# A layernorm, dilated-attention and gated-MLP kernel: logits matmuls issued in pairs, a second PSUM bank pair for the down projection, and weight loads in 27 pieces

## Chip, cores, metric

One core of one Trainium2 chip. The time is device microseconds of one execution. The granted TensorE clock is listed with every run and plays a part below. All runs here count as fast; where it matters I split them further, by granted clock: 0.999 or 1.000 ("full clock") and 0.994 or 0.995 ("dropped").

## The reference, cut to what matters

Both branches take the layernorm of the same x, and the result is their sum with x. S = 2048, D = 640, F = 1536, 32 heads of 20, a window of 8 positions at distance 2.

```python
x = A_x
xn = _layernorm(x, axis=-1)
return x + _A_ref(xn, A_wqkv, A_wo) + _B_ref(xn, B_w_gate, B_w_up, B_w_down)

# _A_ref, per head: each position looks at itself and 7 earlier ones, 2 apart
logits = jnp.einsum("bhsd,bhswd->bhsw", q, kg) * scale      # kg, vg: gathered k, v
attn = _softmax(jnp.where(mask, logits, -1e9), axis=-1)
o = jnp.einsum("bhsw,bhswd->bhsd", attn, vg)                # then @ wo
# _B_ref: no activation
h = (xn @ w_gate) * (xn @ w_up);  out = h @ w_down
```

## The kernel before

A small scheduler lists operations in program order for each engine and derives the semaphore waits from what each reads and writes. An engine works through its own list in order. The work is one long list for TensorE: QKV; then logits steps, with gate and up groups of the MLP between them; then softmax, with more gate/up groups and the first four down tiles beside it; then PV, with the rest of the MLP between its matmuls; then a tail.

VectorE multiplies Q by a shifted K (`qk_prod`, three buffers). TensorE sums the products over each head with four matmuls against a 0/1 matrix of 32 columns, one for each quarter of S, each in its own 32 columns of the array:

```python
def qk_logits(w, c, slot):
    lb = 6 + (w % 2)
    for jj in range(NJ):                       # NJ = 4
        ... e.matmul(PS[32 * jj:32 * jj + 32, lb, :], G[:, c, :],
                     PRODW[:, slot, jj * JB:(jj + 1) * JB],
                     start=(c == 0), stop=(c == NCH - 1), tile_position=(0, 32 * jj))
# the logits stage: 40 steps, one gate or up group (5 matmuls of 128x128x512) after each
qk_prod(order[0][0], order[0][1], 0)
for i, (w, c) in enumerate(order):
    if i + 1 < len(order):
        w2, c2 = order[i + 1]
        qk_prod(w2, c2, (i + 1) % NPW)         # NPW = 3
    qk_logits(w, c, i % NPW)
    next_glu()
```

A down tile (24 matmuls, 640 columns out) always uses PSUM banks 4 and 5. Ahead of PV, ScalarE empties them (`bev`, L552) into a buffer that shares its memory with the softmax's sums:

```python
def glu_down_q(st, jg, q):                     # cut
    ... e.matmul(PS[:, 4, :], HT4[:, hb, m, rows], WD[:, m, 0:512], ...)      # q = 0, 1
    ... e.matmul(PS[:, 5, 0:128], HT4[:, hb, m, rows], WD[:, m, 512:D], ...)  # q = 2
def glu_xb(st, jg):                            # cut
    if not pv_started[0]:
        ... e.activation(xbl(t), b_view(), ACT.Copy)     # b_view(): banks 4 and 5
    else:
        ... e.tensor_tensor(xbl(t), b_view(), XST[:, slot, :], ALU.add)
# softmax: five pieces, five MLP groups after each
for pc in softmax_pieces():
    pc()
    for _ in range(5):
        next_glu()
```

The MLP and output weights are four loads, issued after the first quarter of QKV.

Of the kernel before, what the change touches and what calls it, by code (L numbers as in the profile page):

```python
# [7 lines left out]
ALU = mybir.AluOpType  # L8
# [3 lines left out]
D = 640  # L12
# [166 lines left out]
def psk(b):  # L179
    return [("ps", b, q) for q in range(4)]  # L180


def build_kernel(nc, A_x, A_wqkv, A_wo, B_x, B_w_gate, B_w_up, B_w_down, out, dbg=None):
# [34 lines left out]
    def xbl(t):  # L218
        return XBL_LO[:, t, :] if t < 8 else XBL_HI[:, t - 8, :]
# [21 lines left out]
    def tp_view(u):  # L241
        return PS[:, u, :].bitcast(BF16)[:, 0:NCH * 128].rearrange("p (c f) -> p c f", c=NCH)

    def b_view():
        return PS[:, 4:6, :].rearrange("p a f -> p (a f)")[:, 0:D]

    xhbm = A_x[0]
    ohbm = out[0]
# [43 lines left out]
                                                      wqkv_src[:, :, g3 * D:(g3 + 1) * D]))(g3),  # L292
               writes=[("wqkv", g3)], lane=f"sp_wqkv{g3}", name=f"ld_wqkv{g3}")

    def glu_weight_loads():
        op("sp", lambda e: e.dma_start(WG[:], B_w_gate.rearrange("(c p) n -> p c n", p=128)),
           writes=[("wg",)], lane="sp_wg", name="ld_wg")
        op("sp", lambda e: e.dma_start(WU[:], B_w_up.rearrange("(c p) n -> p c n", p=128)),
           writes=[("wu",)], lane="sp_wu", name="ld_wu")
        op("sp", lambda e: e.dma_start(WD[:], B_w_down.rearrange("(c p) n -> p c n", p=128)),  # L300
           writes=[("wd",)], lane="sp_wd", name="ld_wd")
        op("sp", lambda e: e.dma_start(WO[:], A_wo.rearrange("(c p) n -> p c n", p=128)),
           writes=[("wo",)], lane="sp_wo", name="ld_wo")

    def ln_stats(t):
        slot = t % NXS
# [153 lines left out]
    def g_bank(k):  # L460
        if pv_started[0]:
            return 2
        if ktx_free[0]:
            return (2, 3, 1, 6)[k % 4]
        return (2, 3, 1)[k % 3]

    def e_bank(i):
# [2 lines left out]
    def u_bank(k):  # L470
        if pv_started[0]:
            return (4, 5)[k % 2]
        if ktx_free[0]:
            return (4, 5, 7, 0)[k % 4]
        return (4, 5, 0)[k % 3]

    def slots(k):
        if ktx_free[0]:
# [3 lines left out]
    def glu_gate(m, jg):  # L482
        k = glu_pair[0]
        gb = g_bank(k)
        gsx, usx, gk, uk, extra = slots(k)
        gs = k % NGX
        for c in range(NCH):
            op("pe", (lambda c: lambda e: e.matmul(PS[:, gb, :], WG[:, c, m * 128:(m + 1) * 128],  # L488
                                                 XNT[:, c, jg * JB:(jg + 1) * JB],
                                                 start=(c == 0), stop=(c == NCH - 1)))(c),  # L490
               reads=[("wg",), ("xnt", c, jg)], writes=psk(gb), name=f"gate{m}_{jg}_{c}")
        op("act", lambda e: e.activation(gsx[:, gs, :], PS[:, gb, :], ACT.Copy),  # L492
           reads=psk(gb) + extra, writes=[gk], name=f"gev{m}_{jg}")

    h_pending = []
    H_DEFER = 2

    def flush_h(keep=0):
        while len(h_pending) > keep:
            h_pending.pop(0)()  # L500

    def flush_h_block(jg):
        flush_h()

    def glu_up(m, jg):
        k = glu_pair[0]
        glu_pair[0] += 1
        ub = u_bank(k)
        gsx, usx, gk, uk, extra = slots(k)
        gs = k % NGX  # L510
        hb = jg % 2
        for c in range(NCH):
            op("pe", (lambda c: lambda e: e.matmul(PS[:, ub, :], WU[:, c, m * 128:(m + 1) * 128],  # L513
                                                 XNT[:, c, jg * JB:(jg + 1) * JB],
                                                 start=(c == 0), stop=(c == NCH - 1)))(c),
               reads=[("wu",), ("xnt", c, jg)], writes=psk(ub), name=f"up{m}_{jg}_{c}")
        if pv_started[0]:
            op("dve", lambda e: e.tensor_copy(usx[:, gs, :], PS[:, ub, :]),
               reads=psk(ub) + extra, writes=[uk], name=f"ucp{m}_{jg}")
        else:  # L520
            op("act", lambda e: e.activation(usx[:, gs, :], PS[:, ub, :], ACT.Copy),  # L521
               reads=psk(ub) + extra, writes=[uk], name=f"uev{m}_{jg}")

        def h_op(m=m, jg=jg, gs=gs, hb=hb, gsx=gsx, usx=usx, gk=gk, uk=uk):
            op("dve", lambda e: e.tensor_tensor(HT4[:, hb, m, :], usx[:, gs, :], gsx[:, gs, :], ALU.mult),
               reads=[uk, gk, ("ra",)], writes=[("ht", hb, m)], name=f"h{m}_{jg}")
        h_pending.append(h_op)
        flush_h(keep=H_DEFER)

    def glu_down_q(st, jg, q):  # L530
        hb = jg % 2
        t = 4 * jg + st
        rows = slice(st * 128, (st + 1) * 128)
        if q < 2:
            for m in range(6 * q, 6 * q + 6):
                op("pe", (lambda m: lambda e: e.matmul(PS[:, 4, :], HT4[:, hb, m, rows], WD[:, m, 0:512],  # L536
                                                     start=(m == 0), stop=(m == NF - 1)))(m),
                   reads=[("ht", hb, m), ("wd",)], writes=psk(4), name=f"down{t}_0_{m}")
        else:
            for m in range(NF):  # L540
                op("pe", (lambda m: lambda e: e.matmul(PS[:, 5, 0:128], HT4[:, hb, m, rows], WD[:, m, 512:D],  # L541
                                                     start=(m == 0), stop=(m == NF - 1)))(m),
                   reads=[("ht", hb, m), ("wd",)], writes=psk(5), name=f"down{t}_1_{m}")

    xb_constructed = set()

    def glu_xb(st, jg):
        t = 4 * jg + st
        slot = t % NXS
        xb_constructed.add(t)  # L550
        if not pv_started[0]:
            op("act", lambda e: e.activation(xbl(t), b_view(), ACT.Copy),  # L552
               reads=psk(4) + psk(5) + xbl_alias_keys(t), writes=[("xbl", t)], name=f"bev{t}")
            op("dve", lambda e: e.tensor_tensor(xbl(t), xbl(t), XST[:, slot, :], ALU.add),
               reads=[("xbl", t), ("xst", slot)], writes=[("xbl", t)], name=f"xb{t}")
        else:
            op("dve", lambda e: e.tensor_tensor(xbl(t), b_view(), XST[:, slot, :], ALU.add),  # L557
               reads=psk(4) + psk(5) + [("xst", slot)] + xbl_alias_keys(t), writes=[("xbl", t)], name=f"xb{t}")

    units = [(w, c, j) for j in range(NJ) for c in range(NCH) for w in range(W)]  # L560
    unit_idx = {u: i for i, u in enumerate(units)}
# [36 lines left out]
    def wo_half(t, nb):  # L598
        j = t // 4
        u = t % 2  # L600
        rows = slice(t * TS, (t + 1) * TS)
        cols = slice(nb * DHALF, (nb + 1) * DHALF)
        if pv_all_issued[0]:
            ab = (ABANK, 0, 3)[wo_ctr[0] % 3]
        else:
            ab = ABANK
        wo_ctr[0] += 1
        for c in range(NCH):
            op("pe", (lambda c: lambda e: e.matmul(PS[:, ab, 0:DHALF], QOT[:, c, rows], WO[:, c, cols],  # L609
                                                 start=(c == 0), stop=(c == NCH - 1)))(c),  # L610
               reads=[("ot", c, j), ("wo",)], writes=psk(ab), name=f"wo{t}_{nb}_{c}")
        op("dve", lambda e: e.tensor_tensor(FOUT[:, u, cols], PS[:, ab, 0:DHALF], xbl(t)[:, cols], ALU.add),
           reads=psk(ab) + [("xbl", t)], writes=[("fout", u, nb)], name=f"fin{t}_{nb}")
        if nb == 1:
            op("sp", lambda e: e.dma_start(ohbm[rows, :], FOUT[:, u, :]),
               reads=[("fout", u, 0), ("fout", u, 1)], writes=[("hbm", t)],
               lane=f"sp_fin{u}", name=f"odma{t}")
# [5 lines left out]
    def ln_tile_pre(t):  # L623
        ln_stats(t)
        g = ln_scalars(t, t + 1)
        ln_apply(t, g)
        if t + 8 < NT:
            x_load(t + 8)

    def ln_tile_pe(t):  # L630
        pe_tr(t)
# [14 lines left out]
    for j in range(NJ):  # L646
# [8 lines left out]
                dump("qt0", QOT[:, :, 0:JB], [("qt", c, 0) for c in range(NCH)])  # L655
                dump("kt0", KTP[:, :, 0:PAD + JB], [("kt", c, 0) for c in range(NCH)] + [("kt", c, -1) for c in range(NCH)])
        if j == 0:
            glu_weight_loads()
    for t in pend_pre:
        ln_tile_pre(t)  # L660
    for t in pend_pe:
# [17 lines left out]
    def add_dn(jg):  # L679
        for st in range(4):  # L680
            glu_groups.append(("dn", st, jg, 0))
            glu_groups.append(("dn", st, jg, 1))
            glu_groups.append(("dn", st, jg, 2))

    add_pairs(0)
    add_pairs(1)
    add_dn(0)
# [6 lines left out]
    def run_glu(it):  # L694
        k = it[0]
        if k == "xr":
            x_reload(it[1])
            return 0.0
        if k == "gate":
            glu_gate(it[1], it[2]); return 1.1  # L700
        if k == "up":
            glu_up(it[1], it[2]); return 1.1
        if k == "dn":
            flush_h_block(it[2])
            glu_down_q(it[1], it[2], it[3])
            if it[3] == 2:
                glu_xb(it[1], it[2])
                return 0.7
            return 1.3
        return 0.0  # L710
# [9 lines left out]
                return r  # L720
        return None

    step = 0
    order = [(w, c) for w in range(W) for c in range(NCH)]
    qk_prod(order[0][0], order[0][1], 0)
    for i, (w, c) in enumerate(order):
        if i + 1 < len(order):
            w2, c2 = order[i + 1]
            qk_prod(w2, c2, (i + 1) % NPW)
        qk_logits(w, c, i % NPW)  # L730
        next_glu()
    ktx_barrier()

    dump("logits", LOG[:, :, :].rearrange("p w s -> p (w s)"), [("log", w, j) for w in range(W) for j in range(NJ)])
# [112 lines left out]
```

## Time and profile before

| | before |
|---|---|
| time, median of 4 runs | 361.0 us (360.43 to 362.96) |
| span of the profiled run, granted clock | 358.3 us, 1.000 |
| TensorE busy | 338.2 us (94%) |
| first QKV matmul | 16.09 us |
| logits stage: first logits matmul (85.46) to the end of its 40 groups (145.98) | 60.52 us |
| softmax stage, to the first PV matmul (178.85) | 32.87 us |
| PV, to its last matmul (338.81) | 159.96 us |
| tail, to the end | 19.49 us |

TensorE is busy 94% of the time, so a change helps only where TensorE stands idle or where its matmuls stand further apart than their work needs. The prediction below shows the lines for this: a table of stretches, the timeline of the logits stage, and the holes between down tiles.

### The profile page before, as it was taken

How to read it: one execution, taken by the hardware profiler on the slowest of the kernel's cores; microseconds unless marked ns; L12 is line 12 of the kernel's file. 1: busy time of each engine (PE TensorE's matmuls, PEld its weight loads, DVE VectorE, ACT ScalarE, POOL GpSimd, SP SyncE). 2: the span in 40 equal slices, each digit the busy share in tenths (PEclk: the TensorE clock that was granted, in tenths of full speed). 3: DMA queues.
4: the chain of work that ended last, by engine and by line, in shares of the span. 5: the costliest groups of instructions: out<-in, count | busy, mean ns of one | idle time of the engine just before them, and what ended most of it. 6: DMA issues, size and time to landing. Idle time of an engine off the chain costs nothing.

```text
span 358.3 us, 4796 instructions
## 1 busy us (share of the span) xinstructions
PE 338.2 (94%) x1884; PEld 158.8 (44%) x1884; DVE 212.5 (59%) x439; ACT 202.8 (57%) x362; POOL 16.6 (5%) x43
## 2 busy tenths in 40 slices
PE   1499999999999999978999999999999999999996
PEld 1245454444333333434444445554445444555553
DVE  5746440033999998635475676556667676656633
ACT  4467676554444444561477776556776777556400
POOL 7000000002000200001100000000000000000000
PEclk9999999999999999999999999999999999999999
DMA  7929900002000110001100000111000100010011
GB/s 217 307 69 399 340 4 0 0 2 65 8 2 0 33 43 2 0 0 38 37 1 2 0 0 20 54 40 37 0 20 18 38 2 0 1 38 18 20 37 38
DMA packets 10982, 17.47 MB, mean 49 GB/s; under 512 B 928, under 2 KB 9120, under 8 KB 10960
## 3 DMA queue, kind: packets, MB, share of 16 engines
q1 hardware_dynamic: 10096, 14.42, 11.9%
q0 software_dynamic: 864, 2.75, 2.5%
q8 instruction: 15, 0.25, 0.3%
q14 instruction: 7, 0.06, 0.1%
HBM read 14.42 MB, written 2.62 MB: 48 GB/s over the span
## 4 chain that ended last, share of the span: by engine, by line
PE 91%; DVE 5%; ACT 3%; DMA 1%; issue 1%; DVEq 0%; ACTq 0%
PE PS L355 19%; PE PS L488 15%; PE PS L513 14%; PE PS L536 11%; PE PS L573 10%; PE PS L589 10%; PE PS L609 5%; PE PS L380 4%; PE PS L541 3%; ACT LOG L413 1%; PE PS L340 1%; DVE KTP L557 1%; DVE STATS L308 1%; DVE STATS L310 1%; DMA XST<-in_A_x_dram 1%; DVE PRODW L416 1%
## 5 line engine op out<-in xcount | busy, mean ns | idle before, releaser
L575 ACT ACTIVATE ES<-PS 128x512 bf16<-128x512 f32 x160 | 88.3, 598 | 39.5 <-PE PS L573 39.5
L581 DVE TENSOR_TENSOR PB<-ES,VTP 128x512 bf16<-128x512 bf16 x160 | 67.1, 424 | 56.6 <-ACT ES L575 52.6
L355 PE MATMUL PS<-XNT,RA 128*128 128x512 bf16 x300 | 68.2, 385 | 1.1 <-DVE XNT L346 1.1
L374 DVE TENSOR_TENSOR PRODW<-QOT,KTP 128x2048 bf16<-128x2048 bf16 x40 | 48.8, 1225 | 31.2 <-ACT KTP L368 19.6
L573 PE MATMUL PS<-LOG,GTZ 128*128 128x512 bf16 x160 | 60.5, 379 | 0.0
L589 PE MATMUL PS<-PB,IDENT 128*128 128x512 bf16 x160 | 60.5, 379 | 0.0
L513 PE MATMUL PS<-XNT,WU 128*128 128x512 bf16 x240 | 59.8, 380 | 0.0
L488 PE MATMUL PS<-XNT,WG 128*128 128x512 bf16 x240 | 59.8, 380 | 0.0
L536 PE MATMUL PS<-WD,RA 128*128 128x512 bf16 x192 | 46.1, 379 | 4.7 <-ACT PRODW L552 4.2
L355 PEld LDWEIGHTS PS<-XNT,RA 128*128 128x128 bf16 x300 | 29.2, 99 | 35.0 <-issue 3.2
L513 PEld LDWEIGHTS PS<-XNT,WU 128*128 128x128 bf16 x240 | 21.9, 98 | 28.0 <-issue 4.5
L488 PEld LDWEIGHTS PS<-XNT,WG 128*128 128x128 bf16 x240 | 21.8, 98 | 27.9 <-issue 4.5
L536 PEld LDWEIGHTS PS<-WD,RA 128*128 128x128 bf16 x192 | 18.4, 98 | 26.6 <-ACT PRODW L552 4.7
L609 PE MATMUL PS<-WO,QOT 128*128 128x320 bf16 x160 | 27.0, 299 | 0.1
L492 ACT ACTIVATE KTP<-PS 128x512 bf16<-128x512 f32 x28 | 16.7, 597 | 11.8 <-PE PS L488 11.8
L589 PEld LDWEIGHTS PS<-PB,IDENT 128*128 128x128 bf16 x160 | 15.6, 98 | 17.1 <-DVE PB L581 2.3
L573 PEld LDWEIGHTS PS<-LOG,GTZ 128*128 128x128 bf16 x160 | 15.6, 98 | 15.3 <-ACT ES L575 0.3
L492 ACT ACTIVATE ES<-PS 128x512 bf16<-128x512 f32 x20 | 11.9, 597 | 16.4 <-PE PS L488 16.4
L521 ACT ACTIVATE PB<-PS 128x512 bf16<-128x512 f32 x20 | 11.9, 597 | 16.4 <-PE PS L513 16.4
L609 PEld LDWEIGHTS PS<-WO,QOT 128*128 128x128 bf16 x160 | 15.5, 98 | 10.7 <-ACT QOT L592 0.5
L340 PE MATMUL PS<-IDENT,XNS 128*128 128x128 bf16 x80 | 8.4, 247 | 11.4 <-ACT XNS L332 11.4
L332 ACT ACTIVATE XNS<-XST,NB,RSTD 128x640 bf16<-128x640 bf16 x16 | 14.7, 919 | 6.8 <-DVE NB L324 6.8
(61 smaller groups left out, 246.6 us busy)
## 6 DMA issues: line engine op xcount, KB each, us to landing
XST<-in_A_x_dram SPq DMA_DIRECT2D x16, 160.0 KB, 3.6
XST<-in_A_x_dram POOLq DMA_DIRECT2D x16, 160.0 KB, 2.5
out_dram<-FOUT SPq DMA_DIRECT2D x16, 160.0 KB, 1.8
RA<-in_A_wqkv_dram SPq DMA_DIRECT2D x3, 800.0 KB, 10.4
WG<-in_B_w_gate_dram SPq DMA_DIRECT2D x1, 1920.0 KB, 9.0
WU<-in_B_w_up_dram SPq DMA_DIRECT2D x1, 1920.0 KB, 13.4
WD<-in_B_w_down_dram SPq DMA_DIRECT2D x1, 1920.0 KB, 18.3
WO<-in_A_wo_dram SPq DMA_DIRECT2D x1, 800.0 KB, 19.7
```

The source lines that it names most:

```text
L332: op("act", lambda e: e.activation(XNS[:, u, :], XST[:, slot, :], ACT.Identity, bias=NB[:, t:t + 1], scale=RSTD[:, t:t + 1]), reads=[("xst ...
L355: op("pe", (lambda c: lambda e: e.matmul(PS[:, kb, :], WQKV[:, c, m * 128:(m + 1) * 128], XNT[:, c, j * JB:(j + 1) * JB], start=(c == 0), ...
L374: op("dve", lambda e: e.tensor_tensor(PRODW[:, slot, :], QOT[:, c, :], KTP[:, c, lo:lo + S], ALU.mult), reads=rk, writes=[("prod", slot)], ...
L488: op("pe", (lambda c: lambda e: e.matmul(PS[:, gb, :], WG[:, c, m * 128:(m + 1) * 128], XNT[:, c, jg * JB:(jg + 1) * JB], start=(c == 0), ...
L492: op("act", lambda e: e.activation(gsx[:, gs, :], PS[:, gb, :], ACT.Copy), reads=psk(gb) + extra, writes=[gk], name=f"gev{m}_{jg}")
L513: op("pe", (lambda c: lambda e: e.matmul(PS[:, ub, :], WU[:, c, m * 128:(m + 1) * 128], XNT[:, c, jg * JB:(jg + 1) * JB], start=(c == 0), ...
L536: op("pe", (lambda m: lambda e: e.matmul(PS[:, 4, :], HT4[:, hb, m, rows], WD[:, m, 0:512], start=(m == 0), stop=(m == NF - 1)))(m), reads ...
L573: op("pe", lambda e: e.matmul(PS[:, eb, :], GTZ[:, j, c, :], LOG[:, w, :], start=True, stop=True), reads=[("gtz", j)] + [("log", w, jq) fo ...
L575: op("act", lambda e: e.activation(ES[:, es, :], PS[:, eb, :], ACT.Copy), reads=psk(eb), writes=[("es", es)], name=f"Eev{w}_{c}_{j}")
L581: op("dve", lambda e: e.tensor_tensor(PB[:, pb, :], ES[:, es, :], VTP[:, c, lo:lo + JB], ALU.mult), reads=rk, writes=[("pb", pb)], name=f" ...
L589: op("pe", lambda e: e.matmul(PS[:, ob, :], IDENT[:], PB[:, pb, :], start=(w == 0), stop=(w == W - 1)), reads=[("ident",), ("pb", pb)], wr ...
L609: op("pe", (lambda c: lambda e: e.matmul(PS[:, ab, 0:DHALF], QOT[:, c, rows], WO[:, c, cols], start=(c == 0), stop=(c == NCH - 1)))(c), re ...
```

## The change

Four intentions: logits two by two, so that the array changes less often between 32-column and 128-column matmuls, with products issued two steps ahead; a second bank pair (6 and 7) for every other down tile, ahead of PV and in the tail; three banks each for gate and up where there were four; and the weights in 27 pieces, early, between the x loads. A function that interleaves down tiles with gate/up, and a flag that holds back h multiplies, are added but never used.

```diff
-    def b_view():
-        return PS[:, 4:6, :].rearrange("p a f -> p (a f)")[:, 0:D]
+    def b_view(bb):
+        return PS[:, bb:bb + 2, :].rearrange("p a f -> p (a f)")[:, 0:D]
...
-    def glu_weight_loads():                          # 4 loads
+    wchunks = [...]                                  # 5 + 5 + 12 + 5 loads
+    def weight_chunk_loads(n):
...
     def g_bank(k):                                   # u_bank likewise
-        if ktx_free[0]:
-            return (2, 3, 1, 6)[k % 4]
         return (2, 3, 1)[k % 3]
+    def b_banks(t):
+        if t not in b_banks_of:
+            b_banks_of[t] = (6 if pv_all_issued[0] and t % 2 else 4) if pv_started[0] else (4 if t % 2 else 6)
+        return b_banks_of[t]
...
         if t + 8 < NT:
             x_load(t + 8)
+            weight_chunk_loads(3)
...
     qk_prod(order[0][0], order[0][1], 0)
+    qk_prod(order[1][0], order[1][1], 1)
     for i, (w, c) in enumerate(order):
-        if i + 1 < len(order):
-            w2, c2 = order[i + 1]
-            qk_prod(w2, c2, (i + 1) % NPW)
+        if i + 2 < len(order):
+            w2, c2 = order[i + 2]
+            qk_prod(w2, c2, (i + 2) % NPW)
         qk_logits(w, c, i % NPW)
-        next_glu()
+        if i % 2 == 1:
+            next_glu()
+            next_glu()
```

More of the change, by code (lines that the diff above doesn't have):

```diff
@@ L293, in weight_loads @@
                writes=[("wqkv", g3)], lane=f"sp_wqkv{g3}", name=f"ld_wqkv{g3}")
-    def glu_weight_loads():
-        op("sp", lambda e: e.dma_start(WG[:], B_w_gate.rearrange("(c p) n -> p c n", p=128)),
-           writes=[("wg",)], lane="sp_wg", name="ld_wg")
-        op("sp", lambda e: e.dma_start(WU[:], B_w_up.rearrange("(c p) n -> p c n", p=128)),
-           writes=[("wu",)], lane="sp_wu", name="ld_wu")
-        op("sp", lambda e: e.dma_start(WD[:], B_w_down.rearrange("(c p) n -> p c n", p=128)),
-           writes=[("wd",)], lane="sp_wd", name="ld_wd")
-        op("sp", lambda e: e.dma_start(WO[:], A_wo.rearrange("(c p) n -> p c n", p=128)),
-           writes=[("wo",)], lane="sp_wo", name="ld_wo")
+    wchunks = []
+    wg_src = B_w_gate.rearrange("(c p) n -> p c n", p=128)
+    wu_src = B_w_up.rearrange("(c p) n -> p c n", p=128)
+    wd_src = B_w_down.rearrange("(c p) n -> p c n", p=128)
+    wo_src = A_wo.rearrange("(c p) n -> p c n", p=128)
+    for c in range(NCH):
+        wchunks.append((("wg", c), (lambda c: lambda e: e.dma_start(WG[:, c, :], wg_src[:, c, :]))(c)))
+        wchunks.append((("wu", c), (lambda c: lambda e: e.dma_start(WU[:, c, :], wu_src[:, c, :]))(c)))
+    for m in range(NF):
+        wchunks.append((("wd", m), (lambda m: lambda e: e.dma_start(WD[:, m, :], wd_src[:, m, :]))(m)))
+    for c in range(NCH):
+        wchunks.append((("wo", c), (lambda c: lambda e: e.dma_start(WO[:, c, :], wo_src[:, c, :]))(c)))
+    def weight_chunk_loads(n):
+        while n > 0 and wchunks:
+            key, fn = wchunks.pop(0)
+            op("sp", fn, writes=[key], lane=f"sp_{key[0]}{key[1]}", name=f"ld_{key[0]}{key[1]}")
+            n -= 1
     def ln_stats(t):
@@ L472, in u_bank @@
             return (4, 5)[k % 2]
-        if ktx_free[0]:
-            return (4, 5, 7, 0)[k % 4]
         return (4, 5, 0)[k % 3]
+    b_banks_of = {}
+    def b_banks(t):
+        if t not in b_banks_of:
+            b_banks_of[t] = (6 if pv_all_issued[0] and t % 2 else 4) if pv_started[0] else (4 if t % 2 else 6)
+        return b_banks_of[t]
     def slots(k):
@@ L490, in glu_gate @@
                                                  start=(c == 0), stop=(c == NCH - 1)))(c),
-               reads=[("wg",), ("xnt", c, jg)], writes=psk(gb), name=f"gate{m}_{jg}_{c}")
+               reads=[("wg", c), ("xnt", c, jg)], writes=psk(gb), name=f"gate{m}_{jg}_{c}")
         op("act", lambda e: e.activation(gsx[:, gs, :], PS[:, gb, :], ACT.Copy),
@@ L496, in build_kernel @@
     H_DEFER = 2
+    h_hold = [False]
     def flush_h(keep=0):
@@ L515, in glu_up @@
                                                  start=(c == 0), stop=(c == NCH - 1)))(c),
-               reads=[("wu",), ("xnt", c, jg)], writes=psk(ub), name=f"up{m}_{jg}_{c}")
+               reads=[("wu", c), ("xnt", c, jg)], writes=psk(ub), name=f"up{m}_{jg}_{c}")
         if pv_started[0]:
@@ L527, in glu_up @@
         h_pending.append(h_op)
-        flush_h(keep=H_DEFER)
+        if not h_hold[0]:
+            flush_h(keep=H_DEFER)
     def glu_down_q(st, jg, q):
@@ L533, in glu_down_q @@
         rows = slice(st * 128, (st + 1) * 128)
+        bb = b_banks(t)
         if q < 2:
             for m in range(6 * q, 6 * q + 6):
-                op("pe", (lambda m: lambda e: e.matmul(PS[:, 4, :], HT4[:, hb, m, rows], WD[:, m, 0:512],
+                op("pe", (lambda m: lambda e: e.matmul(PS[:, bb, :], HT4[:, hb, m, rows], WD[:, m, 0:512],
                                                      start=(m == 0), stop=(m == NF - 1)))(m),
-                   reads=[("ht", hb, m), ("wd",)], writes=psk(4), name=f"down{t}_0_{m}")
+                   reads=[("ht", hb, m), ("wd", m)], writes=psk(bb), name=f"down{t}_0_{m}")
         else:
             for m in range(NF):
-                op("pe", (lambda m: lambda e: e.matmul(PS[:, 5, 0:128], HT4[:, hb, m, rows], WD[:, m, 512:D],
+                op("pe", (lambda m: lambda e: e.matmul(PS[:, bb + 1, 0:128], HT4[:, hb, m, rows], WD[:, m, 512:D],
                                                      start=(m == 0), stop=(m == NF - 1)))(m),
-                   reads=[("ht", hb, m), ("wd",)], writes=psk(5), name=f"down{t}_1_{m}")
+                   reads=[("ht", hb, m), ("wd", m)], writes=psk(bb + 1), name=f"down{t}_1_{m}")
     xb_constructed = set()
@@ L550, in glu_xb @@
         xb_constructed.add(t)
+        bb = b_banks(t)
         if not pv_started[0]:
-            op("act", lambda e: e.activation(xbl(t), b_view(), ACT.Copy),
-               reads=psk(4) + psk(5) + xbl_alias_keys(t), writes=[("xbl", t)], name=f"bev{t}")
+            op("act", lambda e: e.activation(xbl(t), b_view(bb), ACT.Copy),
+               reads=psk(bb) + psk(bb + 1) + xbl_alias_keys(t), writes=[("xbl", t)], name=f"bev{t}")
             op("dve", lambda e: e.tensor_tensor(xbl(t), xbl(t), XST[:, slot, :], ALU.add),
@@ L556, in glu_xb @@
         else:
-            op("dve", lambda e: e.tensor_tensor(xbl(t), b_view(), XST[:, slot, :], ALU.add),
-               reads=psk(4) + psk(5) + [("xst", slot)] + xbl_alias_keys(t), writes=[("xbl", t)], name=f"xb{t}")
+            op("dve", lambda e: e.tensor_tensor(xbl(t), b_view(bb), XST[:, slot, :], ALU.add),
+               reads=psk(bb) + psk(bb + 1) + [("xst", slot)] + xbl_alias_keys(t), writes=[("xbl", t)],
+               name=f"xb{t}")
     units = [(w, c, j) for j in range(NJ) for c in range(NCH) for w in range(W)]
@@ L610, in wo_half @@
                                                  start=(c == 0), stop=(c == NCH - 1)))(c),
-               reads=[("ot", c, j), ("wo",)], writes=psk(ab), name=f"wo{t}_{nb}_{c}")
+               reads=[("ot", c, j), ("wo", c)], writes=psk(ab), name=f"wo{t}_{nb}_{c}")
         op("dve", lambda e: e.tensor_tensor(FOUT[:, u, cols], PS[:, ab, 0:DHALF], xbl(t)[:, cols], ALU.add),
@@ L657, in build_kernel @@
         if j == 0:
-            glu_weight_loads()
+            weight_chunk_loads(len(wchunks))
     for t in pend_pre:
@@ L683, in add_dn, with add_dn_interleaved @@
             glu_groups.append(("dn", st, jg, 2))
+    def add_dn_interleaved(jg, jn):
+        glu_groups.append(("hold", True))
+        for st in range(4):
+            for q in range(3):
+                glu_groups.append(("dn", st, jg, q))
+            glu_groups.append(("gate", st, jn))
+            glu_groups.append(("up", st, jn))
+        glu_groups.append(("hold", False))
+        for st in range(4):
+            glu_groups.append(("xr", 4 * jn + st))
+        for m in range(4, NF):
+            glu_groups.append(("gate", m, jn))
+            glu_groups.append(("up", m, jn))
     add_pairs(0)
@@ L698, in run_glu @@
             return 0.0
+        if k == "hold":
+            h_hold[0] = it[1]
+            if not it[1]:
+                flush_h()
+            return 0.0
         if k == "gate":
@@ L703, in run_glu @@
         if k == "dn":
-            flush_h_block(it[2])
+            if not h_hold[0]:
+                flush_h_block(it[2])
             glu_down_q(it[1], it[2], it[3])
@@ L721, in next_glu @@
         return None
-    step = 0
     order = [(w, c) for w in range(W) for c in range(NCH)]
     qk_prod(order[0][0], order[0][1], 0)
+    qk_prod(order[1][0], order[1][1], 1)
     for i, (w, c) in enumerate(order):
-        if i + 1 < len(order):
-            w2, c2 = order[i + 1]
-            qk_prod(w2, c2, (i + 1) % NPW)
+        if i + 2 < len(order):
+            w2, c2 = order[i + 2]
+            qk_prod(w2, c2, (i + 2) % NPW)
         qk_logits(w, c, i % NPW)
-        next_glu()
+        if i % 2 == 1:
+            next_glu()
+            next_glu()
     ktx_barrier()
```

## The prediction

> **What bounds the kernel now.** I read the page first (busy shares and the 40 slices), then a table of stretches that I cut where the program changes stage, then the timeline of each stretch that holds a part of the change. The table, with stretch in us, its length, and the busy time of PE, PEld, DVE, ACT and POOL in it:
>
> ```profile
> 0.00:16.00 16.00, 3.57 (x25) 2.25 (x25) 10.64 (x41) 7.52 (x13) 7.11 (x17) 1.00 0.85 266
> 16.00:58.00 42.00, 41.91 (x229) 20.42 (x230) 19.73 (x72) 29.39 (x55) 0.00 (x0) 1.00 0.52 184
> 58.00:85.60 27.60, 27.60 (x132) 12.38 (x130) 3.50 (x3) 15.59 (x29) 0.00 (x0) 1.00 0.00 1
> 85.60:146.10 60.50, 60.50 (x361) 20.49 (x358) 50.75 (x56) 27.75 (x48) 5.04 (x17) 1.00 0.07 23
> 146.10:179.00 32.90, 28.70 (x168) 14.23 (x166) 18.74 (x21) 14.35 (x19) 2.27 (x5) 1.00 0.07 20
> 179.00:338.00 159.00, 159.00 (x854) 79.09 (x852) 101.97 (x236) 107.65 (x200) 2.14 (x4) 1.00 0.05 17
> 338.00:358.30 20.30, 16.93 (x127) 9.90 (x125) 7.18 (x12) 0.60 (x1) 0.00 (x0) 1.00 0.11 39
> ```
>
> The stages are layernorm, QKV (two rows), logits with gate/up between them, softmax with the first down tiles, PV with the rest of the GLU, and the tail. TensorE sets the time from 16 us on, at full clock (the 1.00), and is free only at the start, in the softmax stretch and in the tail. In PV it has 159.00 of 159.00 us, so nothing there can be won by moving waits. A "busy" PE can still lose time between matmuls, and the timeline of the logits stage shows where (start, duration, what, count):
>
> ```profile
> 141.53 0.40 PE L380 MATMUL PS<-PRODW,G 128*32 128x512 bf16 x4
> 141.86 1.25 PE L513 MATMUL PS<-XNT,WU 128*128 128x512 bf16 x5
> 143.04 0.40 PE L380 MATMUL PS<-PRODW,G 128*32 128x512 bf16 x4
> 143.38 1.25 PE L488 MATMUL PS<-XNT,WG 128*128 128x512 bf16 x5
> 144.56 0.40 PE L380 MATMUL PS<-PRODW,G 128*32 128x512 bf16 x4
> 144.89 1.25 PE L513 MATMUL PS<-XNT,WU 128*128 128x512 bf16 x5
> 145.98 1.24 PE L488 MATMUL PS<-XNT,WG 128*128 128x512 bf16 x5
> ```
>
> A step (four logits matmuls, side by side in 32-column tiles, then one gate or up group) takes 143.04 - 141.53 = 1.51 us. Without logits a group takes 145.98 - 144.89 = 1.09, or 1.08 in the chain's pieces after 146 us. Pure work is 1.08 + 0.216 (four logits matmuls at once) = 1.296. So 0.22 us of each step is neither. It is the change between 128-column and 32-column matmuls: 1.19 - 1.08 = 0.11 on the way back, and the same on the way in. The waits agree, since before each logits group the weight load, which otherwise runs ahead, stands still:
>
> ```profile
> PEld PS L380 <- issue: 17.0, 40, 0.4
> DVE PRODW L374 <- PE PS L380: 11.3, 19, 6.1
> ```
>
> The second line says that VectorE waits for TensorE here, not the reverse. In the softmax stretch the timeline shows PE standing between the first down tiles:
>
> ```profile
> 157.20 0.83 PE L541 MATMUL PS<-WD,RA 128*128 128x128 bf16 x12
> 160.65 2.76 PE L536 MATMUL PS<-WD,RA 128*128 128x512 bf16 x12 [2.61 <-ACT PRODW L552]
> 163.25 0.83 PE L541 MATMUL PS<-WD,RA 128*128 128x128 bf16 x12
> 164.88 2.76 PE L536 MATMUL PS<-WD,RA 128*128 128x512 bf16 x12 [0.80 <-ACT PRODW L552]
> 167.48 0.83 PE L541 MATMUL PS<-WD,RA 128*128 128x128 bf16 x12
> 169.11 2.76 PE L536 MATMUL PS<-WD,RA 128*128 128x512 bf16 x12 [0.80 <-ACT PRODW L552]
> ```
>
> All four tiles use PSUM banks 4 and 5, so each must wait until ScalarE (L552) has emptied them. Twelve narrow matmuls hold the array 0.68 us, so the true holes are 160.65 - 157.88 = 2.77, 164.88 - 163.93 = 0.95 and 169.11 - 168.16 = 0.95: 4.67 us. The bracket counts less because it starts at a matmul's end, not where the next could start.
>
> **What the Trainium skill says.** (1) "TensorEngine Tiling (Array Packing)", Key Properties: changing the tiling mode, not just the tile, drains TensorE, and different tiles can load weights and multiply in parallel. The trace agrees: 0.22 us a round trip, and four logits matmuls in one 0.40 us piece. (2) "TensorE: Matmul & The Clock Gate", What happens when you issue a matmul, gives about 216 ns between matmuls of 512 columns. The trace has 135 QKV matmuls in 29.14 us, 215.9 ns each. (3) "DMA: Bandwidth & Descriptors", Queues, rings and completion order: an engine takes one ring's descriptors in order. The trace agrees as far as it goes: the four weight loads, issued together, landed after 9.0, 13.4, 18.3 and 19.7 us, one behind the other. (4) "PSUM — Partial Sum Buffer", Rules for kernel authors: what is read while a matmul runs should be in another bank. That is what a second bank pair buys.
>
> **The change, part by part.**
> - *Weight loads.* Four loads become 27, three behind each reload of x, so they start near 7 us instead of about 27. Their first use is the gate group at 85.8 us, long after the old ones landed, so nothing is gained. They stand behind the QKV weights in the same queue, but ahead of x tiles 9 to 15. The three QKV loads were issued by 6.7 us and the last took 12.0 us, so they end near 17.6. Nine chunks of 384 KB (3.5 MB at the 400 GB/s of slice 3, 9 us) put x tile 11 near 28 us, and its statistics ran at about 34. The later chunks are 160 KB. I count 0, with at most 1 us of loss. TensorE meets 27 load waits instead of 4, all long satisfied.
> - *Logits two by two.* 40 steps become 20 of two logits groups, then gate and up. A pair took 2 x 1.515 = 3.03 us. With one round trip in place of two it takes 10 x 0.216 + 2 x 0.216 + 0.22 = 2.81. That is 20 x 0.22 = 4.4 us less, if two logits groups follow each other without a new drain. If the second shows its weight load (0.11), 2.2 us. Can VectorE follow? Three products in a row took 3.50 us, so 1.14 apart; the product before an h multiply is also 1.14, and the h 0.37: 2.65 us a pair. It keeps 0.16 us in hand. The third product buffer was used already, as three products ran before the stage, so the deeper prefetch only keeps the old lead for the new order.
> - *Two bank pairs for down tiles before PV.* Tiles 0 and 2 go to banks 6 and 7, which the last logits have left; 1 and 3 to 4 and 5. Counted from the last logits group, tile 0 ends at 14.7 us and tile 1 at 18.1. Bank 6 is free when ScalarE has copied tile 0, which waits for the softmax sum (2.28 us) behind the last h multiply and the exponential (3.61 us). ScalarE has the exponential from 8.7 to 12.3, three evictions to 13.8, the h to 14.2, the sum to 16.5, the copy to 17.2. That is 0.9 us before tile 2 wants it. All 4.67 us should go.
> - *Three gate and three up banks* where there were four each: banks of the groups issued during the exponential were emptied before it. No cost.
> - *Bank pair 6/7 for tiles 13 and 15.* Two waits for L557 in the tail:
>
> ```profile
> 343.97 0.84 PE L609 MATMUL PS<-WO,QOT 128*128 128x320 bf16 x5
> 345.05 1.47 PE L536 MATMUL PS<-WD,RA 128*128 128x512 bf16 x6 [0.24 <-DVE KTP L557]
> ```
>
> Five matmuls of 320 columns hold the array 0.68, so 345.05 - 344.65 = 0.40 us goes, twice: 0.8 us.
> - The interleaved down list and its hold flag are defined but never put in the list of work: 0.
>
> Sum: 4.4 + 4.67 + 0.8 = 9.9 us, nearly all on TensorE's chain, which sets the end. PV follows at once, its input being ready: I have the attention weights done 3 us before its first matmul, as now.
>
> **The rivals.**
> - *Logits pairs do not run together.* Each group still pays its own weight load, or waits for its product. For it: no place in this trace has two such groups in a row, so I cannot read the gap. Against it: the tiles load at the same time, and the page ties the drain to a change of mode. Saving 2.2 + 4.67 + 0.8 = 7.7 us, time 353.3.
> - *VectorE becomes the bound of the logits stage.* 2.65 of 2.81 us is close, and a product may not start before its buffer's logits are done (0.6 us after they start). A handoff of 0.1 or 0.2 us in each pair costs 2 to 4 us: time 353 to 355.
> - *The softmax hole stays.* If the sum comes 0.9 us later than worked out, tile 2 waits in place of tile 1, and 1 to 2 us come back: about 353.
> - *The early weights hold up x.* If chunks delayed the QKV weights or x, the gap before QKV, which ends at 16.1 us, would grow by up to 3 us. The order of the queue speaks against it.
>
> **Range and chances.** The span of 358.3 us less 9.9 is 348.4. The runs' median is 2.7 us above the span, so 351.1. With about a quarter for the first two rivals (a loss of 2 to 3) I say 351.7 us. Low end: every term holds and some unseen wait goes too, 349.5. High end: the logits give 1 us or less and the softmax hole half returns, 355.0. The 2% line is at 353.8, a gain of 7.2 us. The single rivals land near it, two together go past it: faster 0.78, within 2% 0.21, slower 0.01.
>
> **What would show it.** Right: in the new trace two L380 groups about 0.22 us apart, a pair every 2.8 us, the logits stage near 56 us; no wait of L536 for L552; no wait of L536 for L557 in the tail; the QKV start still at 16.1. Wrong: two L380 groups 0.33 apart or more with a VectorE wait ahead; a hole before down tile 2; DMA as releaser of x statistics after 20 us; new waits of gate or up groups for ScalarE in the exponential.

## The result, and the profile after

The changed kernel takes 351.06 us (median of 10 runs, 350.38 to 351.72) against 361.3 us for the kernel before in the same rounds (15 runs, 360.32 to 363.01). The ratio is 0.9707, with a 95% interval from 0.9686 to 0.9727: faster. A ratio is the mean time of one kernel's fast runs over that of the other's of the same rounds, so not quite the ratio of the medians. The prediction was 351.7 us, within 349.5 to 355.0.

The table of stretches for the changed kernel, cut at the same events as before (stretch, its length, busy time of PE, PEld, DVE, ACT, POOL, then clock, DMA share, GB/s; PE is TensorE's matmuls, PEld its weight loads, DVE VectorE, ACT ScalarE, POOL GpSimd):

```profile
85.60:141.60 56.00, 56.00 (x361) 20.37 (x361) 50.92 (x56) 28.22 (x48) 5.04 (x17) 1.00 0.08 24
141.60:169.90 28.30, 28.30 (x168) 14.32 (x167) 17.85 (x21) 14.34 (x19) 2.26 (x5) 1.00 0.08 24
169.90:328.90 159.00, 159.00 (x854) 79.03 (x852) 101.97 (x236) 107.66 (x200) 2.14 (x4) 1.00 0.05 17
328.90:348.50 19.60, 16.62 (x127) 10.11 (x125) 7.18 (x12) 0.60 (x1) 0.00 (x0) 1.00 0.12 42
```

The softmax stretch now has TensorE busy for all of its 28.30 us. From one landmark to the next, in the two profiled runs:

| stage | before | after | difference |
|---|---|---|---|
| start, to the first QKV matmul | 16.09 | 16.06 | -0.03 |
| QKV | 69.37 | 69.48 | +0.11 |
| logits | 60.52 | 56.10 | -4.42 |
| softmax | 32.87 | 28.15 | -4.72 |
| PV | 159.96 | 159.96 | 0.00 |
| tail | 19.49 | 18.75 | -0.74 |
| span | 358.3 | 348.5 | -9.8 |

The timeline of the changed kernel's logits stage, on TensorE (start, duration, what, count; a bracket would give the idle time before and what ended it):

```profile
133.31 0.62 PE L389 MATMUL PS<-PRODW,G 128*32 128x512 bf16 x8
133.86 1.25 PE L500 MATMUL PS<-XNT,WG 128*128 128x512 bf16 x5
134.94 1.24 PE L526 MATMUL PS<-XNT,WU 128*128 128x512 bf16 x5
136.12 0.62 PE L389 MATMUL PS<-PRODW,G 128*32 128x512 bf16 x8
```

Two logits groups are one piece of 0.62 us, where one took 0.40: the second costs 0.22, one pass of 512 columns and nothing more. The round is 136.12 - 133.31 = 2.81 us. The four down tiles of the softmax stage follow each other without a bracket, that is, without a wait:

```profile
152.87 0.83 PE L556 MATMUL PS<-WD,RA 128*128 128x128 bf16 x12
153.54 2.75 PE L551 MATMUL PS<-WD,RA 128*128 128x512 bf16 x12
156.13 0.83 PE L556 MATMUL PS<-WD,RA 128*128 128x128 bf16 x12
156.80 2.75 PE L551 MATMUL PS<-WD,RA 128*128 128x512 bf16 x12
```

In the tail the two waits for VectorE are gone as well; the same place as the prediction's last fence (there 345.05 - 343.97 = 1.08 us apart, here 0.68):

```profile
334.91 0.84 PE L626 MATMUL PS<-WO,QOT 128*128 128x320 bf16 x5
335.59 1.46 PE L551 MATMUL PS<-WD,RA 128*128 128x512 bf16 x6
```

And the waits around the logits matmuls, to be read against the two lines in the prediction (40 standing weight loads, 17.0 us; VectorE waiting 19 times):

```profile
PEld PS L389 <- issue: 8.1, 19, 0.4
DVE PRODW L383 <- PE PS L389: 7.0, 3, 6.1
```

The standing weight loads are halved, and VectorE has almost stopped waiting for TensorE: it is now nearly as loaded as TensorE is in this stage (50.92 of 56.00 us busy).

### The profile page after: what moved, and what is told of

It is laid out like the page before. It is cut to its first block, busy times and chain, and to the rows that moved or that the text cites. A ratio compares the mean times of both kernels' runs of the same rounds, so it can differ in the third digit from the quotient of the medians.

```text
span 348.5 us, 4822 instructions
## 1 busy us (share of the span) xinstructions
PE 333.0 (96%) x1884; PEld 158.8 (46%) x1884; DVE 211.8 (61%) x439; ACT 203.3 (58%) x362; POOL 16.5 (5%) x43
## 4 chain that ended last, share of the span: by engine, by line
PE 94%; DVE 4%; DMA 1%; ACT 1%; issue 0%; DVEq 0%
PE PS L364 19%; PE PS L500 15%; PE PS L526 15%; PE PS L551 12%; PE PS L590 10%; PE PS L606 10%; PE PS L626 6%; PE PS L389 3%; PE PS L556 3%; PE PS L349 1%; DVE STATS L317 1%; DVE STATS L319 1%; DMA XST<-in_A_x_dram 1%; DVE XNT L355 0%; DVE MV L321 0%; ACT SD L329 0%
## 5 line engine op out<-in xcount | busy, mean ns | idle before, releaser
L526 PEld LDWEIGHTS PS<-XNT,WU 128*128 128x128 bf16 x240 | 23.5, 98 | 28.2 <-ACT PRODW L568 0.2
L606 PEld LDWEIGHTS PS<-PB,IDENT 128*128 128x128 bf16 x160 | 15.6, 98 | 17.1 <-DVE PB L598 2.3
L341 ACT ACTIVATE XNS<-XST,NB,RSTD 128x640 bf16<-128x640 bf16 x16 | 14.7, 920 | 6.8 <-DVE NB L333 6.8
```

Source lines behind the costliest of these rows:

```text
L341: op("act", lambda e: e.activation(XNS[:, u, :], XST[:, slot, :], ACT.Identity, bias=NB[:, t:t + 1], scale=RSTD[:, t:t + 1]), reads=[("xst ...
L526: op("pe", (lambda c: lambda e: e.matmul(PS[:, ub, :], WU[:, c, m * 128:(m + 1) * 128], XNT[:, c, jg * JB:(jg + 1) * JB], start=(c == 0), ...
L606: op("pe", lambda e: e.matmul(PS[:, ob, :], IDENT[:], PB[:, pb, :], start=(w == 0), stop=(w == W - 1)), reads=[("ident",), ("pb", pb)], wr ...
```

## The experiments

The theory: the logits gain is 20 changes of tiling mode and back, 0.22 us each; the softmax gain is the bank wait; the tail gain is two bank waits; nothing else does anything. The rivals: VectorE or the weight load of the second logits group takes the gain, or the parts depend on each other. Three calls, each on its own chip: e1 to e4 (each part alone), e5 to e8, e9 and e10. "Stretch" in this section is the time from the first logits matmul to the first PV matmul in the profiled run: 93.39 us before, 84.25 us after.

| run | median us | ratio to before (95%) | stretch us | runs at dropped clock |
|---|---|---|---|---|
| changed kernel | 351.06 | 0.9707 (0.9686 to 0.9727) | 84.25 | 0 of 10 |
| e1 pairs only | 358.62 | 0.9883 (0.9847 to 0.9920) | 90.67 | 5 of 6 |
| e2 banks only | 356.06 | 0.9828 (0.9797 to 0.9859) | 88.66 | 0 of 6 |
| e3 chunks only | 360.83 | 0.9968 (0.9949 to 0.9988) | 94.97 | 2 of 19 |
| e4 tail only | 360.01 | 0.9971 (0.9950 to 0.9993) | 93.39 | 7 of 22 |
| e5 prefetch 1 | 351.10 | 0.9709 (0.9679 to 0.9738) | 84.25 | 0 of 6 |
| e6 two buffers | 353.51 | 0.9788 (0.9755 to 0.9822) | 87.19 | 0 of 6 |
| e7 triples | 351.00 | 0.9708 (0.9678 to 0.9738) | 84.35 | 0 of 6 |
| e8 quads | 349.52 | 0.9663 (0.9634 to 0.9692) | 82.33 | 0 of 6 |
| e9 no second pair | 357.56 | 0.9889 (0.9858 to 0.9920) | 90.68 | 6 of 6 |
| e10 second pair once | 353.22 | 0.9772 (0.9739 to 0.9805) | 86.19 | 0 of 6 |

In the three calls' 61 runs of the kernel before, 21 had the dropped clock. In the first call, 25 at full clock took 360.78 us on average and 14 dropped ones 363.10.

By the 2% rule the changed kernel, e5, e7 and e8 count as faster than the kernel before, e1, e3, e4 and e9 as the same, and e2, e6 and e10 as unclear. A ratio also depends on how many dropped runs of the kernel before fell into its rounds, so the parts are read from the stretch of the profiled runs, with the clock in view.

### e1: logits pairs alone

The edit is the last hunk of the diff above, on the kernel before.

> The kernel before with the new order of the logits stage alone. Theory (a round trip between 128-column and 32-column matmuls costs 0.22 us, 20 of them go): 4.4 us less than before, stage of 56.1 us, and the hole before the second down tile stays, since its banks are the old ones. It should even shrink, because the softmax starts one group (1.08 us) earlier against TensorE's list: 2.77 us becomes about 1.7 us. So 5.5 us less in all. Rival (the gain of the logits stage needs the rest of the change, or the softmax hole takes it back): 0 to 3 us less.

Measured: 358.62 us. From its first logits matmul to the end of its 40 groups the logits stage took 142.48 - 86.38 = 56.10 us, the same as in the changed kernel and as expected, against 60.52 us before, so the gain of the pairs needs no other part of the change. Two things were not expected. First, the hole did not shrink (157.16 - 154.39 = 2.77 us in the timeline of this run). ScalarE's timeline shows why:

```profile
148.08 0.60 ACT L492 ACTIVATE KTP<-PS 128x512 bf16<-128x512 f32 x1 [0.48 <-PE PS L488]
148.57 3.61 ACT L413 ACTIVATE LOG<-LOG 128x4096 bf16<-128x4096 bf16 x1
```

The exponential (L413) follows at once on the eviction of a gate group, and that waits for TensorE. In ScalarE's list the exponential stands behind it. So everything after it, down to the copy of tile 0, moves with TensorE's own progress and not with the last logits matmul. Second, five of the six runs had a dropped clock, and the profiled one is among them: the down tile after the hole took 4.45 us instead of 2.76. That is 1.69 of the 4.42 us given back: the stretch is 93.39 - 90.67 = 2.72 us shorter. The one run at full clock took 355.76 us, 5.0 less than the full-clock mean of before; being one run, it shows no more than the direction.

### e2: second bank pair ahead of PV alone

```diff
-            return (2, 3, 1, 6)[k % 4]      # with its condition; u_bank likewise
+    def b_banks(t): ...  4 if pv_started[0] or t % 2 else 6
```

> The kernel before with the second bank pair for the four down tiles ahead of PV alone, and with three gate and three up banks. Theory: the three holes of 2.77, 0.95 and 0.95 us go. But the softmax chain now starts 1.08 us later against TensorE's list than in the changed kernel, where the copy of tile 0 ended only 0.54 us before tile 2 wanted its bank; so some 0.5 us of hole may come back before tile 2: 4.1 to 4.7 us less. Rival (three gate and up banks cost waits during the exponential): less than 4 us, with waits of gate or up groups for ScalarE.

Measured: 356.06 us. The stretch is 93.39 - 88.66 = 4.73 us shorter: all of the holes (2.77 + 0.95 + 0.95 = 4.67). No hole came back, for the reason just found in e1: the chain moves with TensorE, so the margin is the same with either order of the logits. Three gate and up banks cost no wait. No run had a dropped clock.

### e3: early weight loads alone

```diff
-        glu_weight_loads()                  # after the first quarter of QKV
+        weight_chunk_loads(3)               # after each reload of x
```

> The kernel before with the 27 early weight loads alone. Theory: within 0.2 us of before, as the loads were hidden and stay so. Rival (the early loads help or hurt the start): QKV would start elsewhere than at 16.1 us, by 0.5 us or more.

Measured: 360.74 us as the mean of its 17 runs at full clock, against 360.78 before: nothing. Its median is 360.83. The profiled run fell among the two with a dropped clock (361.9 us span), and its first QKV matmul came at 16.69 instead of 16.09 us. That one look would have spoken for the rival; the 17 runs do not. The ratio of 0.9968 is below 1 only because fewer of its runs had the dropped clock. This profile is the best view of the drop. The table of stretches around the hole (the clock is the third number from the end), then TensorE's timeline:

```profile
150.00:160.00 10.00, 9.95 (x55) 4.75 (x54) 5.14 (x9) 7.36 (x8) 0.00 (x0) 1.00 0.00 0
160.00:163.00 3.00, 0.38 (x2) 0.13 (x2) 2.17 (x2) 0.70 (x1) 0.00 (x0) 0.91 0.00 0
163.00:165.00 2.00, 2.00 (x6) 0.73 (x5) 0.12 (x1) 0.00 (x0) 0.54 (x1) 0.50 0.08 15
165.00:167.00 2.00, 2.00 (x11) 0.87 (x10) 0.00 (x0) 0.00 (x0) 0.00 (x0) 0.79 0.20 67
```

```profile
159.20 0.83 PE L550 MATMUL PS<-WD,RA 128*128 128x128 bf16 x12
162.65 4.33 PE L545 MATMUL PS<-WD,RA 128*128 128x512 bf16 x12 [2.62 <-ACT PRODW L561]
```

Cut more finely, the clock is at one half from 162.44 to 165.86 us, so the drop begins within the hole and lasts 3.41 us; 12 matmuls take 4.33 us instead of 2.76.

### e4: bank pair 6/7 in the tail alone

```diff
+            b_banks_of[t] = 6 if pv_all_issued[0] and t % 2 else 4
```

> The kernel before with banks 6 and 7 for down tiles 13 and 15 alone. Theory: 0.7 to 0.8 us less, all in the tail. Rival (the tail is set by VectorE's last additions and not by these two waits): 0.

Measured: the tail of the profiled run is 18.72 us instead of 19.49, so 0.77 less, as expected. At full clock the means are 359.79 us (15 runs) and 360.78, a difference of 0.99.

### e5: products one step ahead in the changed kernel

```diff
-    qk_prod(order[1][0], order[1][1], 1)
-        if i + 2 < len(order): ... qk_prod(w2, c2, (i + 2) % NPW)
+        if i + 1 < len(order): ... qk_prod(w2, c2, (i + 1) % NPW)
```

> The changed kernel with the products issued one step ahead, as before, instead of two. Theory (VectorE runs ahead as far as its three buffers let it, whatever the place in the list): same as the changed kernel, within 0.2 us, about 351.1. Rival (the deeper prefetch is what keeps VectorE ahead of the pairs): each pair waits for its second product, 1 us or more, 10 to 20 us slower than the changed kernel.

Measured: 351.10 us, and the same stretch to the hundredth, 84.25 us. The deeper prefetch does nothing. VectorE's list holds the products in nearly the same order either way, and what lets it run ahead is the number of buffers.

### e6: two product buffers in the changed kernel

```diff
-            qk_prod(w2, c2, (i + 2) % NPW) ... qk_logits(w, c, i % NPW)
+            qk_prod(w2, c2, (i + 1) % 2)   ... qk_logits(w, c, i % 2)
```

> The changed kernel with products one step ahead and only two product buffers in use. This measures how close VectorE is to the bound. By my count the second product of the next pair starts about 1.74 us after a pair's first logits group and ends at 2.97, and its logits are due at 3.03: 0 to 0.2 us per pair, 0 to 4 us slower than the changed kernel. If VectorE had been the bound already, 10 us or more slower.

Measured: 353.51 us; the stretch is 87.19 us, 2.94 more than with three, or 0.15 us per pair. TensorE's logits matmuls now wait for the products (waits of this run):

```profile
DVE PRODW L383 <- PE PS L389: 11.6, 11, 7.2
PEld PS L389 <- DVE PRODW L383: 3.9, 9, 0.4
```

The first line is VectorE waiting for a buffer (7.2 us of it ahead of the stage), the second TensorE waiting for the product. So VectorE is close to the bound in pairs, but with three buffers not at it.

### e7: three logits groups in a row

```diff
-        if i % 2 == 1:
+        if i % 3 == 2:                      # three groups of gate/up instead of two
```

> The changed kernel with three logits groups, then three gate or up groups: 14 round trips instead of 20. Theory (cost per change of mode): 6 x 0.22 = 1.3 us less than the changed kernel, 349.7. VectorE needs 3 x 1.14 + 1.5 x 0.37 = 3.98 us of a round of 4.11 and has three buffers, so its third product ends about when it is due; if it comes late, the gain is lost and some more: 351 to 354. Rival (cost per logits group, not per change of mode): no gain.

Measured: 351.00 us, no gain (stretch 84.35 against 84.25). TensorE's timeline has both kinds of rounds:

```profile
97.57 0.83 PE L389 MATMUL PS<-PRODW,G 128*32 128x512 bf16 x12
98.33 1.25 PE L526 MATMUL PS<-XNT,WU 128*128 128x512 bf16 x5
...
101.67 1.11 PE L389 MATMUL PS<-PRODW,G 128*32 128x512 bf16 x12
102.94 1.03 PE L500 MATMUL PS<-XNT,WG 128*128 128x512 bf16 x4 [0.16 <-issue]
106.06 0.83 PE L389 MATMUL PS<-PRODW,G 128*32 128x512 bf16 x12
```

The first round is 101.67 - 97.57 = 4.10 us, what the theory has (4.11); the next is 106.06 - 101.67 = 4.39, since its third product comes late (a piece of 1.11 us where three groups need 0.83). VectorE waits for a buffer and then has too little time. Over the 13 rounds that is (140.03 - 85.25) / 13 = 4.21 us, and the 1.3 us are lost again. Alone, this run doesn't tell the theory from its rival.

### e8: four in a row, and a fourth buffer

```diff
+    PROD4 = RA[:, 10240:12288]              # free until h tiles 8 to 11 of the second block
-        if i % 2 == 1:
+        if i % 4 == 3:                      # four groups of gate/up instead of two
```

> The changed kernel with four logits groups, then four gate or up groups, and a fourth product buffer in a part of RA that is not in use yet: 10 round trips instead of 20. Theory: 10 x 0.22 = 2.2 us less than the changed kernel, 348.9, if VectorE follows; it needs 4 x 1.14 + 2 x 0.37 = 5.30 us of a round of 5.40, so any handoff shows. Rival (VectorE becomes the bound): the round is 5.5 us or more and the gain shrinks to 1 us or turns.

Measured: 349.52 us, faster than both kernels. The stretch is 82.33 us, 1.92 less than in the changed kernel, of the 2.2 foreseen. Means of the same rounds are 349.31 us here and 350.94 for e5, which equals the changed kernel in time. Most rounds are as worked out, 97.57 - 92.17 = 5.40 us:

```profile
92.17 0.83 PE L396 MATMUL PS<-PRODW,G 128*32 128x512 bf16 x12
92.83 0.39 PE L396 MATMUL PS<-RA,G 128*32 128x512 bf16 x4
...
97.57 0.83 PE L396 MATMUL PS<-PRODW,G 128*32 128x512 bf16 x12
```

With the kernel before and the changed kernel this makes three points of one line: 40, 20 and 10 round trips, at 1.515, 2.81 / 2 = 1.405 and 5.40 / 4 = 1.35 us per step. Above the pure work of 1.296 us that is 0.22, 0.11 and 0.05 us: it falls with the number of round trips. A cost per logits group would have stayed at 0.22.

### e9: no second pair ahead of PV in the changed kernel

```diff
-            ... if pv_started[0] else (4 if t % 2 else 6)
+            ... if pv_started[0] else 4
```

> The changed kernel with all four down tiles ahead of PV on banks 4 and 5 again; the rest as changed. Theory: the three holes of 2.77, 0.95 and 0.95 us are back, 4.7 us slower than the changed kernel at full clock, about 355.5; and, since the long hole is back, some runs show the granted clock of 0.995 and are some 2.3 us longer still, as runs of the kernel before, e1, e3 and e4 did and no run of the changed kernel, e2, e5 to e8 did. Rival (the clock drops have nothing to do with the hole): no run at 0.995.

Measured: 357.56 us; all six runs had a dropped clock. The stretch is 6.43 us longer than in the changed kernel: 4.67 for the holes, and 1.76 more, nearly all of it the slow down tile (4.45 us instead of 2.76). The hole and the drop came back together.

### e10: second pair for tile 0 only

```diff
-            ... if pv_started[0] else (4 if t % 2 else 6)
+            ... if pv_started[0] else (6 if t == 0 else 4)
```

> The changed kernel with the second bank pair for tile 0 only (tiles 1 to 3 on banks 4 and 5). Tile 1 then does not wait, tiles 2 and 3 do, 0.95 us each. Theory: 1.9 us slower than the changed kernel, about 353.0, and no run at 0.995, as only the hole of 2.77 us brings the clock down. Rival (any hole in this stage does it): runs at 0.995 here too.

Measured: 353.22 us, a stretch 1.94 us longer than in the changed kernel, and no run at a dropped clock. The two short waits are in TensorE's timeline, and the tiles after them take the normal 2.76 us:

```profile
157.45 2.76 PE L551 MATMUL PS<-WD,RA 128*128 128x512 bf16 x12 [0.80 <-ACT PRODW L568]
...
161.68 2.76 PE L551 MATMUL PS<-WD,RA 128*128 128x512 bf16 x12 [0.80 <-ACT PRODW L568]
```

So the long hole goes with the clock drop, and short ones do not. Over all runs with a listed clock, kernels with the hole of 2.77 us (before, e1, e3, e4, e9) had it dropped in 41 of 114; those without (the changed kernel, e2, e5 to e8, e10) in none of 46.

## Why the prediction was right

**The logits pairs (predicted -4.4, measured -4.42).** Right in size and in cause. The choice between 4.4 and 2.2 us could not be read from the trace of before. The changed kernel's pieces of 0.62 us settle it, and e1 and e8 confirm the cost per round trip. (The prediction has its two halves of 0.11 us the wrong way round: the 1.19 us end with the change into 32 columns.) Whether TensorE drains in these 0.11 us, or only cannot load the next weights ahead (the standing weight loads fell from 40 to 19 with the round trips), no run here tells apart.

**VectorE as the next bound (a rival).** Not at two by two. The 0.16 us in hand were real, but small: e6 and e7 both use them up, and e8 gets through with a fourth buffer. The statement that the deeper prefetch does nothing was right (e5).

**The softmax holes (predicted -4.67, measured -4.72 in the stage, -4.73 in e2, 4.67 within e9).** Right. Only the margin was smaller than worked out: the copy of tile 0 ended at 156.26 us and tile 2 began at 156.80, 0.54 us later instead of 0.9. ScalarE's chain came out as foreseen: the copy ended 17.1 us after the last logits group (at 139.15, the second of the piece at 138.93), and 17.2 were predicted. TensorE's side was put too late: the prediction gave a down tile 3.4 us (14.7 to 18.1), and it takes 156.80 - 153.54 = 3.26. My expectations for the hole in e1 and e2 were wrong for another reason: there I counted from the last logits group as if it set the pace, and these runs showed that TensorE's gate groups do, through ScalarE's list.

**Tail (predicted -0.8, measured -0.74 and, in e4, -0.77), early loads (predicted 0, e3: 360.74 against 360.78), three banks (predicted 0, e2).** Right.

**The time itself (351.1 us before the allowance for rivals, 351.7 with it; measured 351.06).** The gain was worked out; that the time came so close is partly luck. The 2.7 us put between span and median came from four runs of the kernel before, and the profiled execution itself was 2.0 us above its span (360.31 and 358.3). In the changed kernel the median is 2.6 us above the profiled span because that execution (350.42 us) was among its fastest.

**What the prediction missed.** The clock, twice. It took the full clock for granted from 16 us on ("the 1.00"). In the trace of before the first QKV matmuls stand 0.427 us apart until 19.08 us, and 0.216 after; the record of the clock begins only there, and the view shows 1.00 where nothing is recorded. And 21 of 61 runs of the kernel before had the drop after the long hole, which the change removes. In the profiled runs the drop costs 1.6 to 1.7 us, the excess of the slow tile. So the steps that I worked out are right, and the mean gain has one more term, 21/61 of 1.7, or some 0.6 us: the ratio of 0.9707 is 10.6 us (361.68 to 351.06), while the profiled runs, both at full clock, differ by 9.8. The drop is also why the parts alone fall short of the whole: e1 and e2 shorten the stretch by 2.72 and 4.73 us, together 7.45, and the whole change by 9.14; the 1.69 between is the drop in the profiled run of e1.

**When the drop comes.** The kept traces of the five runs with the long hole say more (us):

| run | full clock from | the hole | step of 3.413 us that holds most of it | idle in that step | half clock from |
|---|---|---|---|---|---|
| before | 19.08 | 157.88 to 160.65 | 159.03 to 162.44 | 1.62 | none |
| e4 | 20.94 | 158.75 to 161.52 | 157.47 to 160.89 | 2.14 | none |
| e3 | 22.50 | 159.88 to 162.65 | 159.03 to 162.44 | 2.56 | 162.44 |
| e1 | 20.97 | 154.39 to 157.16 | 154.09 to 157.50 | 2.77 | 157.50 |
| e9 | 20.63 | 154.23 to 157.00 | 153.75 to 157.16 | 2.77 | 157.16 |

From its rise to the drop the clock was full for 136.53 us (e1, e9) or 139.95 us (e3), that is 40 or 41 times 3.413 us, and each drop lasts 3.41 us. So in these traces the clock changes in steps of 3.413 us counted from its rise, and it dropped where 2.56 us or more of one step were idle, not where 2.14 were. The time of the rise differs from run to run, and in all twelve traces QKV takes 67.86 to 67.88 us plus half of the time between its first matmul and the rise, in dropped runs (70.1 to 70.8 us) and in full ones (69.4 in before, 70.3 in e4, 70.7 in e8) alike. The three profiled dropped runs all rose late. So the rest of the 2.2 us by which dropped runs are slower on average is most likely this longer QKV and no cost of the drop.

The pairs bring the hole forward by 4.42 us, which is not a whole number of steps, so it falls differently into them. An estimate from these numbers, with the rise equally likely anywhere in the 3.41 us after 18.68 us (the earliest seen, in e10) and the limit between 2.14 and 2.55 us: a drop in 6 to 30% of the runs with single logits groups and in 63 to 89% with pairs. The runs had it in 30 of 102 (before, e3, e4) and 11 of 12 (e1, e9). No run moved the hole within a step on purpose, so this is read from five traces and not tested.

**What stays open.** Where between 2.14 and 2.56 us the limit lies, and why e3 had the drop in only 2 of 19 runs when the kernel before, with the same hole, had it in 14 of 39 of the same call; chance is not excluded.

## What to carry to other kernels

Group small-tile matmuls, so that the array changes mode as seldom as the producer's buffers allow: divide the cost of a round trip by the group size, and check that the producer keeps up. Give an accumulator a second bank pair where TensorE stands waiting for its eviction; measure the hole from where the next matmul could start. And look at the list of clocks of all runs, not only the profiled one: a hole can cost more than its length (here up to 1.7 us on top of 2.77).

## What the Trainium skill lacked or had wrong

- "TensorEngine Tiling (Array Packing)", Key Properties, says that a change of mode drains TensorE, but gives no cost. Here a round trip between 128x128 and 128x32 cost 0.22 us, with 512-column matmuls on both sides; a second group in the same mode cost only its 0.22 us of columns.
- "TensorE: Matmul & The Clock Gate", Why this matters for your kernels, warns of idle gaps of more than about 3 us, since one window of idle brings the clock back to half; What's actually happening gives a free-running window of about 3.4 us. The steps of 3.413 us agree. But here a gap of 2.77 us was enough: the clock dropped where 2.56 us or more of one step were idle, and not where 2.14 were. In the three profiled runs with a drop it stayed at half for 3.41 us, at a cost of 1.6 to 1.7 us; 41 of 114 runs with the gap had a drop, and none of 6 with gaps of 0.95 us alone (e10).
- No page seen here says that the same gap can drop the clock in few or in most runs, depending on where it falls among these steps: with the hole 4.42 us earlier it was 11 of 12 runs in place of 30 of 102.
